# Batch 0 of a fused attention and two-MLP kernel: dividing by the softmax sums before or behind the value products

## The chip, the cores and the metric

The kernel runs on one core of a Trainium2 chip. The metric is the device time in microseconds of one execution. A trace of one profiled execution names the engines PE (TensorE, matrix products; PEld is its weight load), DVE (VectorE), ACT (ScalarE), POOL (GpSimd) and SP (it issues the DMAs here). Each engine works through its own queue strictly in order.

## What is computed

Three stages follow each other, for 2 batches of 768 tokens and a width of 512. The first is an attention over a local window and over block summaries of the keys and values (8 heads of 64). The second is an MLP on shifted tokens with a squared ReLU and a sigmoid gate. The third mixes over tokens and over channels. The change lies in the attention and touches nothing else of this:

```python
scores_all = np.concatenate([scores_l_m, scores_s], axis=-1)   # 768 local (masked) + 24 summaries
scores_all = scores_all - np.max(scores_all, axis=-1, keepdims=True)
a = np.exp(scores_all)
a = a / (np.sum(a, axis=-1, keepdims=True) + 1e-09)
v_all = np.concatenate([v, v_sum], axis=2)
return np.matmul(a, v_all).astype(np.float32)
```

The division may be made on `a`, or on the product with the values: both give the same sum.

## The kernel before

The attention works on tiles of 128 queries, six for each batch, and each tile has two halves `e` of four heads (a head is 64 rows of the 128). In batch 0 a unit of work is one half of one tile, so there are 12 units; in batch 1 a unit is a whole tile. A unit goes through four functions:

- `s_stage`: 8 score products on PE into a PSUM bank (`sp`, line 308); on DVE the mask, with the row's extreme as a by-product (line 321, four for a unit); on ACT the exponential, with the row's sum `den` (line 323, four for a unit).
- `n_stage`: on DVE `den + 1e-9` and its reciprocal (lines 331 and 332); on POOL four multiplications `pe * 1/den` (line 334).
- `t_stage`: four transposes on PE into a bank `pt` (line 340; two such banks) and one copy of the bank to `PT` in SBUF, by DVE in batch 0 and by ACT in batch 1 (lines 345 and 343).
- `v_stage`: 8 value products on PE into the one bank `pv` (line 360); behind the second half of a tile ACT copies `pv` to `xT` (line 367), from which the MLP reads.

`LAGS` says how many units later each of the last three functions of a batch 0 unit is written. A scheduler then sets the final order on each engine, so a change of the code moves work on all of them.

Beside batch 0 the first MLP gets ready. Each of its 16 weight tiles is split into a high and a low part: a shift and a combination on DVE (lines 150 and 156), a scaling and a rounding on ACT (lines 146 and 158), a subtraction on POOL (line 159). `mixed` makes the MLP's input for two tiles of 128 tokens: per 128 channels a product on POOL (`tmp`, line 442) and a combination on DVE (`xk`, line 443), then a rounding on ACT and the low part on DVE (`xl`, line 445). With these PE does the MLP's products (`ko` and `acc`, line 453) between the units of the attention; from batch 1 on they fill its queue. Before batch 1 can score, DVE takes maxima over its keys (`ks`, line 230) and sums over its values (`vrs`, line 252). PE also runs 16 products without use (`spin`, line 532) early on.

Of the kernel before, what the change touches and what calls it, by code (L numbers as in the profile page):

```python
# [9 lines left out]
F32 = mybir.dt.float32  # L10
# [4 lines left out]
ALU = mybir.AluOpType  # L15
# [5 lines left out]
EDGE = WINDOW - 1  # L21
BIG = 1.0e9
KB = 7
LAGS = 1, 2, 3
PEB, PTB, VB = 16, 3, 5
MW = 256
RATIO, NR, RATIO2 = 1.2, 25, 1.8
# [3 lines left out]
SPIN, SPIN_UNITS = 1, 8  # L31
WFIRST = 2
S2COST, S3COST, S4COST = 4, 5, 4
PT_ACT = (1,)
GB = 4
PIN3, PIN4 = 3, 3
PINL = True
# [15 lines left out]
def fused_kernel(ctx, tc, q, k, v, vt, mu, w_k, w_v, w_r, w_t1, w_t2, w_c1, w_c2, out):  # L53
    nc = tc.nc
    B, NT = q.shape[:2]
    S, DM = v.shape[1] - WINDOW * 2, v.shape[2]
    H, D = 8, 64
# [3 lines left out]
    NP = H // 2  # L61
# [14 lines left out]
    def bank(tag, bufs, shape, name):  # L76
        return ps.tile(shape, F32, tag=tag, bufs=bufs, name=name)

    const = pool("const", "left")
    ident = const.tile([128, 128], F32, name="ident")  # L80
# [85 lines left out]
    def in_line(inst):  # L166

        behind(inst, line[-1:])
        line.append(inst)
# [26 lines left out]
    xT = xp.tile([128, KD, B * XB], F32, name="xT")  # L196
    at = pool("at", "right")

    def ahead(n):

        def wrap(fn):
            def run(*args, **kw):
                with tc.high_priority(n) if n else ExitStack():
                    return fn(*args, **kw)
            return run
        return wrap

    state = {}

    def st_of(b):  # L210
        if b not in state:
            state[b] = {"kw": {}, "qT": {}, "vw": {}, "pv": {}}
            state[b]["ks"] = at.tile([128, NP, NB], F32, tag="ks", bufs=2, name="ks")
        return state[b]

# [16 lines left out]
    @ahead(HK)  # L232
    def kw_sums(b, t):
        st = state[b]
        for o in (0, WC - NB):
            nc.gpsimd.tensor_scalar(st["kw"][t][:, :, o:o + NB], st["ks"], 1.0, 1.0, ALU.mult, ALU.mult)
# [17 lines left out]
    @ahead(HR)  # L254
    def v_gather(b):
        st = state[b]
        vp = bank("pt", 2, [128, NP, 128], "vp")
        for p in range(NP):
            nc.tensor.transpose(vp[:NB, p], st["vr"][:, p], ident)
        st["vs"] = at.tile([NB, DM], F32, tag="vs", bufs=1, name="vs")  # L260
        nc.scalar.activation(st["vs"], vp[:NB].rearrange("p g e -> p (g e)"), AF.Copy, scale=1.0 / BLOCK)

    @ahead(HL)
    def vw_load(b, t):
        ws = []
        for half in range(2):
            w = ybuf[:NC, 2 * t + half] if b == 0 else at.tile([NC, DM], F32, tag="vw", bufs=VB, name="vw")
            row, srow = (NB, 0) if half == 0 else (0, NK)
            key = 128 * t + 64 * half
            after(nc.sync.dma_start(w[row:row + NK], v[b, key:key + NK]))  # L270
            ws.append((w, srow))
        st_of(b)["vw"][t] = ws

    def vw_sums(b, t):
        ahead(HV if b or t == 0 else 0)(copy_sums)(b, t)
# [20 lines left out]
    @ahead(HS)  # L296
    def s_stage(b, t, es):
        st = state[b]
        mask = masks[1 if t == 0 else 2 if t == NT - 1 else 0]
        kw, qT = st["kw"][t], st["qT"][t]  # L300
        sps = [bank("s", 2, [128, NP, NC], "sp") for _ in es]
        line.clear()
        for p in range(NP):
            for half in range(2):
                c0 = half * (WC - NC)
                for sp, e in zip(sps[::-1], es[::-1]):
                    r = slice(64 * e, 64 * e + 64)
                    m = nc.tensor.matmul(sp[64 * half:64 * half + 64, p], qT[r, p, 64 * half:64 * half + 64],  # L308
                                         kw[r, p, c0:c0 + NC], start=True, stop=True)
                    if len(es) > 1:  # L310
                        in_line(m)
        if PINL:
            mark.append(m)
        zs = []
        for sp, e in zip(sps, es):
            mn = at.tile([128, NP], F32, tag="mn", bufs=4, name="mn")
            den = at.tile([128, NP], F32, tag="den", bufs=4, name="den")
            P = []
            for p in range(NP):
                pe = at.tile([128, NC], F32, tag="pe", bufs=PEB, name="pe")  # L320
                nc.vector.tensor_tensor_reduce(out=pe, in0=sp[:, p], in1=mask, op0=ALU.add, op1=ALU.min,  # L321
                                               scale=-1.0 / math.sqrt(D), scalar=3.0e38, accum_out=mn[:, p:p + 1])
                nc.scalar.activation(pe, pe, AF.Exp, bias=mn[:, p:p + 1], scale=-1.0, accum_out=den[:, p:p + 1])  # L323
                P.append(pe)
            zs.append({"u": (b, t, e), "P": P, "den": den})
        return zs
# [9 lines left out]
    @ahead(HT)  # L336
    def t_stage(z):
        pt = bank("pt", 2, [128, NP, 128], "pt")
        for p in range(NP):
            nc.tensor.transpose(pt[:NC, p], z["P"][p], ident)  # L340
        z["PT"] = at.tile([NC, NP, 128], F32, tag="PT", bufs=PTB, name="PT")
        if z["u"][0] in PT_ACT:
            nc.scalar.copy(z["PT"], pt[:NC])
        else:
            nc.vector.tensor_copy(z["PT"], pt[:NC])

    @ahead(HV)
    def v_stage(zs):
        b, t, _ = zs[0]["u"]
        st = state[b]  # L350
        if t not in st["pv"]:
            st["pv"][t] = bank("pv", 1, [128, NP, 128], "pv")
        pv = st["pv"][t]
        line.clear()
        for p in range(NP):
            for half in range(2):
                for z in zs[::-1]:
                    e = z["u"][2]
                    h = 2 * p + e
                    m = nc.tensor.matmul(pv[64 * e:64 * e + 64, p, 64 * half:64 * half + 64],  # L360
                                         st["vw"][t][half][0][:, h * D:(h + 1) * D],
                                         z["PT"][:, p, 64 * half:64 * half + 64], start=True, stop=True)
                    if len(zs) > 1:
                        in_line(m)
        if zs[-1]["u"][2] == 1:
            c0 = b * XB + 1 + 128 * t
            nc.scalar.copy(xT[:, :, c0:c0 + 128], pv)

    done_tiles = [0]

    def attention():
        slots = {}
        n0 = 2 * NT
        steps = [(0, t, (e,)) for t in range(NT) for e in range(2)] + [(b, t, (0, 1)) for b in range(1, B) for t in range(NT)]
        for i in range(len(steps) + 1):
            if i < len(steps):
                b, t, es = steps[i]
                zs = s_stage(b, t, es)
                if len(es) == 1:
                    for what, z, lag in zip((n_stage, t_stage, v_stage), (zs[0], zs[0], zs), LAGS):  # L380
                        slots.setdefault(min(i + lag, n0), []).append(((i + lag, lag), what, z))
                else:
                    slots[i + 1] = [((i, 1), n_stage, z) for z in zs] + [((i, 2), t_stage, z) for z in zs] + [((i, 3), v_stage, zs)]
                if i < SPIN_UNITS:
                    spin(SPIN)
                yield 0.95 * len(es)
                if es[-1] == 1 and t + 1 < NT:
                    kw_sums(b, t + 1)
                if t == 0 and es[-1] == 1 - b * (len(es) == 1):
                    if b == 0:  # L390
                        v_gather(b)
                    vw_sums(b, 0)
            for _, what, z in sorted(slots.get(i, ()), key=lambda s: s[0]):
                what(z)
                if what is t_stage:
                    yield 0.43
                elif what is v_stage:
                    yield 0.7 * len(z)
                    done_tiles[0] += len(z) / 2
            if i < len(steps):  # L400
                if 0 in es:
                    if t + 1 < NT and t + 1 not in state[b]["vw"]:
                        vw_load(b, t + 1)
                    if b and t + 2 < NT:
                        q_load(b, t + 2)
                if 1 in es and t + 1 < NT:
                    vw_sums(b, t + 1)
                if b + 1 < B:
                    for e in es:
                        prep_next(b + 1, 2 * t + e)  # L410
# [117 lines left out]
    def spin(n):  # L528

        o = bank("ko", 1, [128, 4, 128], "spin")  # L530
        for _ in range(n):
            after(nc.tensor.matmul(o, ident, ident.unsqueeze(1).to_broadcast([128, 4, 128]), start=True, stop=True))
# [309 lines left out]
```

## Time and profile before

| what | value |
|---|---|
| device time, median of 3 runs | 519.04 us (518.58 to 519.21) |
| the profiled execution, own time | 519.46 us |
| its span in the trace | 517.4 us |
| granted TensorE clock, mean | 0.987 |
| PE busy | 491.9 us (95%) |
| DVE, ACT, POOL busy | 254.8, 203.7, 198.3 us |

The page's second part shows the span in 40 slices of 12.9 us. PE is full from the eighth slice on; before that it has gaps, while DVE and POOL are at 7 to 9 tenths. So the stretch up to about 90 us is one kind of work (batch 0's attention with the weights' splits) and the rest another (PE bound). The trace says at which instruction the one goes over into the other: DVE's first mask of batch 1 at 89.1 us.

### The profile page before, as it was taken

What the parts mean: (1) busy time and instruction counts of PE and PEld (TensorE: products, weight loads), DVE (VectorE), ACT (ScalarE), POOL (GpSimd) and SP (SyncE); (2) the same over time, 40 slices, a digit from 0 to 9 for tenths busy, and PEclk for the clock granted to TensorE, in tenths of its full rate; (3) what the DMA queues carried; (4) which work ended last, traced back from release to release, by engine and by line L of the source; (5) the groups of instructions that cost most, each with busy time, mean ns of one, the idle gap of its engine ahead of it and who ended that gap; (6) DMA issues with size and microseconds to landing.
All of it is one profiled execution on the core that took longest, in us unless ns stands there. A gap on an engine that the chain in (4) does not pass through costs nothing.

```text
span 517.4 us, 7849 instructions
## 1 busy us (share of the span) xinstructions
PE 491.9 (95%) x2968; PEld 398.9 (77%) x2968; DVE 254.8 (49%) x556; ACT 203.7 (39%) x471; POOL 198.3 (38%) x298
## 2 busy tenths in 40 slices
PE   7899687999999999999999999999999999999995
PEld 3457565888888988888867888888888888888884
DVE  3878998733335477587657766343231211311112
ACT  0668445764545645436345344344211110101100
POOL 5587887862655465378423323423100000000000
PEclk9999889899999999999999999999999999999998
DMA  8999941112005700000166351000020000200002
GB/s 269 285 286 353 326 111 33 46 53 84 7 15 209 280 1 1 1 0 2 46 239 236 133 200 42 0 2 0 1 81 1 0 0 1 81 1 0 1 0 81
DMA packets 24196, 45.39 MB, mean 88 GB/s; under 512 B 2112, under 2 KB 11328, under 8 KB 24160
## 3 DMA queue, kind: packets, MB, share of 16 engines
q1 hardware_dynamic: 24160, 44.90, 27.4%
q8 instruction: 23, 0.38, 0.3%
q14 instruction: 13, 0.11, 0.1%
HBM read 41.16 MB, written 3.15 MB: 86 GB/s over the span
## 4 chain that ended last, share of the span: by engine, by line
PE 72%; DVE 10%; DMA 5%; POOL 4%; issue 4%; SPq 2%; ACT 2%; DVEq 0%; POOLq 0%; ACTq 0%
PE o L767 19%; PE go L453 19%; PE ko L453 10%; PE acc L453 9%; PE ro L453 4%; DMA ybuf<-in_v_dram 3%; PE ho L453 3%; PE h L453 2%; PE sp L308 2%; DVE xk L443 2%; DMA wst<-in_moe_w_k_dram 2%; DVE wf L150 2%; PE pv L360 2%; PE pt L340 1%; POOL kl L468 1%
## 5 line engine op out<-in xcount | busy, mean ns | idle before, releaser
L453 PE MATMUL go<-u,w 128*128 128x512 f32 x432 | 106.7, 393 | 0.0
L159 POOL TENSOR_TENSOR w<-wf,w 128x512 fp32r<-128x512 f32 x50 | 66.7, 1337 | 82.4 <-ACT w L158 80.9
L453 PEld LDWEIGHTS go<-u,w 128*128 128x128 f32 x432 | 80.7, 188 | 17.5
L767 PE MATMUL o<-w,gh 128*128 128x512 f32 x288 | 89.0, 395 | 0.0
L682 DVE SCALAR_TENSOR_TENSOR gl<-go,gh 128x512 fp32r<-128x512 f32 x36 | 24.9, 691 | 121.1 <-ACT gh L681 121.0
L453 PE MATMUL ko<-xh,w 128*128 128x256 f32 x384 | 80.5, 295 | 0.0
L681 ACT ACTIVATE gh<-go 128x512 fp32r<-128x512 f32 x36 | 21.6, 599 | 128.7 <-PE go L453 128.7
L453 PEld LDWEIGHTS ko<-xh,w 128*128 128x128 f32 x384 | 64.4, 196 | 2.8 <-issue 0.8
L767 PEld LDWEIGHTS o<-w,gh 128*128 128x128 f32 x288 | 53.9, 188 | 12.1
L453 PE MATMUL acc<-w,kh 128*128 128x512 f32 x192 | 60.1, 400 | 0.6 <-ACT kh L467 0.6
L453 PE MATMUL ko<-xl,w 128*128 128x256 f32 x192 | 56.1, 292 | 2.2 <-DVE xl L445 2.2
L767 PE MATMUL o<-w,gl 128*128 128x512 f32 x144 | 55.4, 394 | 0.0
L158 ACT CAST w<-wf 128x512 fp32r<-128x512 f32 x50 | 31.0, 619 | 54.5 <-DVE wf L156 52.4
L156 DVE SCALAR_TENSOR_TENSOR wf<-wst,wf 128x512 int32<-128x512 int32 x50 | 43.0, 865 | 8.8 <-ACT wst L146 7.0
L323 ACT ACTIVATE pe<-pe,mn 128x120 f32<-128x120 f32 x96 | 36.7, 384 | 25.4 <-DVE mn L321 24.4
L468 POOL TENSOR_TENSOR kl<-rl,kh 128x512 fp32r<-128x512 f32 x24 | 33.1, 1381 | 32.6 <-ACT kh L467 30.9
L442 POOL TENSOR_SCALAR tmp<-xT,oms 128x256 f32<-128x256 f32 x52 | 33.9, 660 | 27.8 <-DVE xk L443 24.6
L334 POOL TENSOR_SCALAR pe<-pe,den 128x120 f32<-128x120 f32 x96 | 39.6, 432 | 12.3 <-DVE den L332 7.1
L443 DVE SCALAR_TENSOR_TENSOR xk<-xT,mus,tmp 128x256 f32<-128x256 f32 x52 | 35.4, 710 | 13.6 <-POOL tmp L442 13.5
L453 PEld LDWEIGHTS acc<-w,kh 128*128 128x128 f32 x192 | 34.4, 188 | 8.0 <-ACT kh L467 1.0
L453 PEld LDWEIGHTS ko<-xl,w 128*128 128x128 f32 x192 | 37.7, 196 | 3.6 <-DVE xl L445 2.4
L453 PE MATMUL acc<-w,kl 128*128 128x512 f32 x96 | 37.3, 404 | 0.5 <-POOL kl L468 0.5
(79 smaller groups left out, 688.6 us busy)
## 6 DMA issues: line engine op xcount, KB each, us to landing
wst<-in_moe_w_ch_dram SPq DMA_DIRECT2D x24, 512.0 KB, 4.8
wst<-in_moe_w_k_dram SPq DMA_DIRECT2D x8, 512.0 KB, 9.6
wst<-in_moe_w_v_dram SPq DMA_DIRECT2D x8, 512.0 KB, 7.1
kw<-in_k_dram SPq DMA_DIRECT2D x12, 320.0 KB, 4.1
wst<-in_moe_w_tok_dram SPq DMA_DIRECT2D x6, 512.0 KB, 7.5
out_dram<-o SPq DMA_DIRECT2D x12, 256.0 KB, 2.1
ybuf<-in_v_dram SPq DMA_DIRECT2D x12, 192.0 KB, 10.9
vw<-in_v_dram SPq DMA_DIRECT2D x12, 192.0 KB, 2.5
```

The source lines that it names most:

```text
L156: nc.vector.scalar_tensor_tensor(wi, top, 3, wi, ALU.logical_shift_left, ALU.bitwise_or)
L158: self.rounded.append(nc.scalar.copy(hi, wf))
L159: nc.gpsimd.tensor_tensor(lo, wf, hi.bitcast(F32), ALU.subtract)
L323: nc.scalar.activation(pe, pe, AF.Exp, bias=mn[:, p:p + 1], scale=-1.0, accum_out=den[:, p:p + 1])
L334: nc.gpsimd.tensor_scalar(z["P"][p], z["P"][p], den[:, p:p + 1], 1.0, ALU.mult, ALU.mult)
L442: nc.gpsimd.tensor_scalar(tmp, xT[:, d, x0 - 1:x0 - 1 + MW], om[:, d:d + 1], 1.0, ALU.mult, ALU.mult)
L443: nc.vector.scalar_tensor_tensor(xk[:, d], xT[:, d, x0:x0 + MW], mu[:, d:d + 1], tmp, ALU.mult, ALU.add)
L453: nc.tensor.matmul(o, l, r, start=(first and i == 0), stop=(last and i == 3 * n - 1))
L468: nc.gpsimd.tensor_tensor(lo, rl, hi.bitcast(F32), ALU.subtract)
L681: nc.scalar.activation(hi, o, AF.Relu)
L682: nc.vector.scalar_tensor_tensor(lo, o, 0.0, hi.bitcast(F32), ALU.max, ALU.subtract)
L767: nc.tensor.matmul(acc[t], l, r, start=(f == 0 and i == 0), stop=(f == nf - 1 and i == 2))
```

## The change

For batch 0 (`LATE`) `n_stage` is no longer called. The exponentials go to the transposes undivided. The two halves of a tile share one tile `dens` of 2 x 4 sums. Behind the value products of a tile DVE adds 1e-9 and takes the reciprocals of all 8 columns at once. PE spreads them: 8 products of a column, repeated 64 times, with the identity give a bank `rb` that holds `1/den` on each head's 64 rows, for each query. `rb` takes one of the two `pt` banks. ACT copies `pv` to `xT` as before, and DVE multiplies `xT` by `rb` in place. The copies `PT` of batch 0's first halves (`e = 0`) go to ACT, those of the second halves stay with DVE; batch 1 keeps all its copies on ACT and its `n_stage`. `LAGS` is one entry shorter.

```diff
-LAGS = 1, 2, 3
+LAGS = 1, 2
+LATE = (0,)
...
-PT_ACT = (1,)
+PT_ACT = ((0, 0), (1, 0), (1, 1))
...
             mn = at.tile([128, NP], F32, tag="mn", bufs=4, name="mn")
-            den = at.tile([128, NP], F32, tag="den", bufs=4, name="den")
+            if b not in LATE:
+                den = at.tile([128, NP], F32, tag="den", bufs=4, name="den")
+            else:
+                if e == 0:
+                    st["den"][t] = at.tile([128, 2, NP], F32, tag="dens", bufs=3, name="dens")
+                den = st["den"][t][:, e]
...
-        if z["u"][0] in PT_ACT:
+        if z["u"][::2] in PT_ACT:
...
-            nc.scalar.copy(xT[:, :, c0:c0 + 128], pv)
+            if b not in LATE:
+                nc.scalar.copy(xT[:, :, c0:c0 + 128], pv)
+            else:
+                den = st["den"].pop(t)
+                nc.vector.tensor_scalar(den, den, 1e-9, None, ALU.add)
+                nc.vector.reciprocal(den, den)
+                rb = bank("pt", 2, [128, NP, 128], "rb")
+                for p in range(NP):
+                    for e in range(2):
+                        nc.tensor.matmul(rb[64 * e:64 * e + 64, p], den[:, e, p:p + 1].to_broadcast([128, D]), ident,
+                                         start=True, stop=True)
+                x = xT[:, :, c0:c0 + 128]
+                nc.scalar.copy(x, pv)
+                nc.vector.tensor_tensor(x, x, rb, ALU.mult)
...
-                    for what, z, lag in zip((n_stage, t_stage, v_stage), (zs[0], zs[0], zs), LAGS):
+                    for what, z, lag in zip((t_stage, v_stage), (zs[0], zs), LAGS):
```

The order on the engines moves with it. POOL's queue in batch 0, before (line numbers are those of each kernel; `pe<-pe,den` is the multiplication of `n_stage`, `w` a weight's low part, `tmp` a part of `mixed`):

```order
L580 TENSOR_SCALAR oms<-mus 128x8
L334 TENSOR_SCALAR pe<-pe,den 128x120 x8
L286 COPY ybuf<-vs 24x512 x5
L334 TENSOR_SCALAR pe<-pe,den 128x120 x4
L159 TENSOR_TENSOR w<-wf,w 128x512
L334 TENSOR_SCALAR pe<-pe,den 128x120 x12
L159 TENSOR_TENSOR w<-wf,w 128x512
```

And the same place of POOL's queue in the changed kernel:

```order
L599 TENSOR_SCALAR oms<-mus 128x8
L287 COPY ybuf<-vs 24x512 x5
L160 TENSOR_TENSOR w<-wf,w 128x512 x3
L461 TENSOR_SCALAR tmp<-xT,oms 128x256 x2
L160 TENSOR_TENSOR w<-wf,w 128x512
L461 TENSOR_SCALAR tmp<-xT,oms 128x256 x2
```

All 48 multiplications of batch 0 are gone from it. On DVE the first multiplication by `rb` stands here, in the changed kernel (tile 0's sums, the copy of its second half's transposes before that):

```order
L151 TENSOR_SCALAR wf<-wst 128x512
L377 TENSOR_SCALAR dens<-dens 128x8
L351 COPY PT<-pt 120x512
L378 RECIPROCAL dens<-dens 128x8
L386 TENSOR_TENSOR xT<-xT,rb 128x4x128
L157 SCALAR_TENSOR_TENSOR wf<-wst,wf 128x512
L327 ISA pe,mn<-sp,mask_163 128x120
```

Behind it in DVE's queue stand a weight and the next unit's masks. On PE, tile 0 of the changed kernel ends so (`pv` are the value products of its two halves, `pt` the transposes of a later unit):

```order
L366 MATMUL pv<-PT,ybuf 64x64 x8
L309 MATMUL sp<-kw,xT 64x120
L366 MATMUL pv<-PT,ybuf 64x64 x8
L382 MATMUL rb<-ident,dens 64x128 x8
L346 MATMUL pt<-ident,pe 120x128 x4
L551 MATMUL spin<-ident 128x512
L309 MATMUL sp<-kw,xT 64x120 x12
```

In the changed kernel 8 units' value products, 4 tiles' `rb` and 9 units' transposes stand in PE's queue ahead of the first `ko` product; before, 10 units' value products and 10 units' transposes did. Of `spin` 15 stand ahead of it, where all 16 did.

## Rows read from the trace of the kernel before

**Rows 1.** The page's head and PE's line of its first part.

```profile
span 517.4 us, 7849 instructions
PE 491.9 (95%) x2968; PEld 398.9 (77%) x2968; DVE 254.8 (49%) x556; ACT 203.7 (39%) x471; POOL 198.3 (38%) x298
```

**Rows 2.** By stretch: length, busy PE, PEld, DVE, ACT, POOL (instructions), PE clock, DMA, GB/s.

```profile
25.00:60.80 35.80, 29.32 (x316) 21.28 (x315) 30.04 (x114) 25.42 (x85) 30.47 (x56) 0.99 1.06 327
60.80:89.10 28.30, 23.71 (x171) 20.03 (x171) 26.58 (x33) 13.61 (x23) 21.56 (x28) 0.89 0.38 96
89.10:517.40 428.30, 418.82 (x2368) 347.87 (x2368) 184.44 (x362) 156.04 (x328) 132.97 (x155) 0.99 0.17 56
```

**Rows 3.** Waits, 36 to 92 us on DVE, 20 to 92 on PE: total, times, longest.

```profile
DVE pe L321 <- PE pt L340: 4.6, 3, 3.4
...
PE pv L360 <- DVE PT L345: 4.2, 4, 1.4
...
PE ko L453 <- DVE xl L445: 2.2, 1, 2.2
```

**Rows 4.** Timelines of POOL, PE and DVE: start, length, instruction, idle time before it.

```profile
30.94 4.82 POOL L334 TENSOR_SCALAR pe<-pe,den 128x120 f32<-128x120 f32 x12
...
35.90 0.60 PE L340 MATMUL pt<-ident,pe 128*120 128x128 f32 x4
...
36.21 0.28 DVE L321 CUSTOM_DVE_ANT_0 pe<-sp,mask 128x120 f32<-128x120 f32 x1 [3.43 <-PE pt L340]
```

**Rows 5.** The chain of waits, 36 to 92 us: start, share of the chain, what.

```profile
36.90 0.61 DVE PT L345
...
46.48 0.08 DVE den L331
...
47.15 0.09 DVE den L332
...
50.88 0.44 DVE xk L443
```

**Rows 6.** Groups by shape: count, busy us, mean ns, idle before; DVE and ACT.

```profile
L626 DVE TENSOR_TENSOR ybuf<-ybuf,ro 128x512 f32<-128x512 f32 x9 | 6.1, 677 | 1.8 <-ACT ro L624 1.8
...
L466 DVE TENSOR_TENSOR rl<-rl 128x512 f32<-128x512 f32 x3 | 3.2, 1065 | 0.0
...
L367 ACT COPY xT<-pv 128x512 f32<-128x512 f32 x6 | 3.5, 579 | 0.9 <-PE pv L360 0.9
```

**Rows 7.** POOL's multiplications of line 334 alone, first stretch: length, busy (count).

```profile
25.00:60.80 35.80, 16.47 (x40) 0.99 1.06 327
```

**Rows 8.** DVE's timeline, then its lines 150 and 443 alone in the first stretch.

```profile
29.29 1.80 DVE L331 TENSOR_SCALAR den<-den 128x4 f32<-128x4 f32 x1
...
37.62 0.42 DVE L150 TENSOR_SCALAR wf<-wst 128x512 int32<-128x512 int32 x1
...
25.00:60.80 35.80, 5.51 (x7) 0.99 1.06 327
...
25.00:60.80 35.80, 2.92 (x4) 0.99 1.06 327
```

**Rows 9.** A weight's two steps on DVE, groups by shape, 0 to 100 us.

```profile
L150 DVE TENSOR_SCALAR wf<-wst 128x512 int32<-128x512 int32 x16 | 12.7, 792 | 1.5 <-POOL w L159 1.5
L156 DVE SCALAR_TENSOR_TENSOR wf<-wst,wf 128x512 int32<-128x512 int32 x16 | 11.8, 743 | 0.2
```

**Rows 10.** PE's timeline: 8 score products, 8 value products, one `spin` (two passes each).

```profile
22.01 1.04 PE L308 MATMUL sp<-kw,xT 64*64 64x120 f32 x16
...
31.69 1.15 PE L360 MATMUL pv<-PT,ybuf 120*64 120x64 f32 x16
...
33.32 1.13 PE L532 MATMUL spin<-ident 128*128 128x512 f32 x2
```

**Rows 11.** The last large load of batch 1: issue on SP, then us from issue to landing.

```profile
59.54 0.48 SPq L244 DMA_DIRECT2D ybuf<-in_vt_dram  x1
...
ybuf<-in_vt_dram SPq DMA_DIRECT2D x2, 768.0 KB, 7.8
```

More of the change, by code (lines that the diff above doesn't have):

```diff
@@ L211, in st_of @@
         if b not in state:
-            state[b] = {"kw": {}, "qT": {}, "vw": {}, "pv": {}}
+            state[b] = {"kw": {}, "qT": {}, "vw": {}, "pv": {}, "den": {}}
             state[b]["ks"] = at.tile([128, NP, NB], F32, tag="ks", bufs=2, name="ks")
```

## The prediction, made before the changed kernel ran

> **What bounds the kernel now.** I read the page first: PE is busy for 95% of the span [rows 1]. The stretches [rows 2] show where its gaps lie; I cut the span at two instructions that both kernels have: the end of DVE's low part `xl` of the first MLP input (60.8 us), without which the MLP's products can't start, and DVE's first mask of batch 1 (89.1 us), which I call T. From T on PE is busy 418.8 of 428.3 us; this is the PE-bound part, and nothing in the change touches its products. From 25.0 us to T DVE is busy 56.6 of 64.1 us. PE counts as busy for 53.0 of them, in the second stretch at a granted clock of 0.89 in the mean, between its two levels of 1.2 and 2.4 GHz. So the time is T plus a PE-bound remainder, and the question is how far T moves, and what is still owed behind it.
>
> Within the first stretch POOL is as full as DVE (30.5 of 35.8 us), and more than half of that, 16.5 us, is the division [rows 7]. It is on the path at least once: twelve multiplications run from 30.94 to 35.76, PE's next transposes start at 35.90 and DVE, which stood for 3.43 us, goes on at 36.21 [rows 4]. In all DVE waits 4.6 us behind such transposes, and PE 4.2 us for DVE's copies `PT` [rows 3]. The chain of waits from 36 us on is mostly DVE work, piece by piece [rows 5].
>
> **DVE's list up to T.** I counted both queues from 25.0 us to the first mask of batch 1; masks, maxima and sums for batch 1, `xl` and the MLP's squares are the same in number.
> - Six of the twelve copies `PT` leave, at 0.61 [rows 5]: -3.7 us.
> - Small steps on `den`: 9 additions and 10 reciprocals before, 5 and 5 (of twice the width) after. At 0.08 and 0.09 [rows 5], with the one addition of 1.80 [rows 8], that was 3.3 us and becomes 0.9: -2.4.
> - Six multiplications by `rb` come. The trace has no such instruction; its bounds are a copy at 0.61 [rows 5] and, above, a product of two tiles in SBUF at 1.07. I take 0.68, the mean of a 128x512 step that also reads one operand from SBUF and one from PSUM [rows 6]: +4.1 (3.7 to 6.4).
> - One weight (0.79 + 0.74 [rows 9]) and two `xk` (0.73 each, 2.92 for four [rows 8]) now stand behind T: -3.0, owed later.
>
> Sum -5.0 us; -1.9 with multiplications at 1.07 and the additions' 1.80 left in (half of that). I keep -5.0.
>
> The addition of 1.80 us was queued while POOL multiplied and split a weight; an uncrowded one takes 0.08 [rows 5, 8]. The Trainium skill ("SBUF — State Buffer", "Who interferes with whom") has a rule for this: VectorE's two-port steps and GpSimd shut each other out for a whole instruction, while a VectorE step with at most one SBUF input stays clear of it. By that rule the multiplication by `rb` runs at the 0.68 end, and the sum is the one taken; by the dearer row it would be 2.3 us more.
>
> **Waits and collisions on DVE.** Of the 4.6 us behind transposes, the 3.43 has POOL's division as its direct cause, and that is gone; the rest I leave: -3.4 (0 to -4.6). Line 150 took 5.51 us for seven, against 0.42 uncrowded: 2.6 too much. `xk` took 2.92 for four, against 0.44: 1.2 too much [rows 5, 8]. Division is 54% of POOL's time there, so I take back 54% of 3.8: -2.0 (0 to -3.8). By DVE alone T moves by -5.0 - 3.4 - 2.0 = -10.4 us.
>
> **PE's list up to the first MLP product.** This caps it. PE was busy 29.3 us from 25.0 to 60.8 [rows 2]. Ahead of the first `ko` the change adds four `rb` of 8 products each, and leaves out two units' value products (1.15 each [rows 10]), one unit's transposes (0.60 [rows 4]) and one `spin` (1.13 [rows 10]). For `rb` the bounds are these. Score products alternate between the two column halves of the array, as `rb` does, and 8 of 120 columns take 1.04. Value products of a unit all use one half, and 8 of 64 columns take 1.15, so 8 of 128 would take 2.30 [rows 10]. I take 1.04, since the alternation is the same: +4.2 - 2.3 - 0.6 - 1.1 = +0.2, and PE, without any gap, gets there at 25.0 + 29.5 = 54.5 us. That is 6.3 us ahead of the 60.8 at which `xl` ended; PE had stood 2.2 us for it [rows 3]. In the second stretch DVE's own list changes by under 0.5 us (three multiplications and two maxima come; weights and `xk` go), so a PE-capped T moves by about -6.5.
>
> The Trainium skill ("TensorEngine Tiling (Array Packing)", "Key Properties") says that tiles of the array work independently, and also that a change of the tiling mode drains the engine. By the first, `rb` costs 1.04 a tile; by the second alone, with its halves in series, 2.30, and the cap would be 59.5. No row shows `rb`.
>
> Between -6.5 and -10.4 I take -8.4. PE's busy time contains modelled ends of matmuls, so 54.5 is on the late side; DVE's sum assumes that nothing new makes it wait, so it is on the early side.
>
> **ACT and the loads.** ACT gets six copies at 0.58 [rows 6], 3.5 us, four of them in a stretch where it is busy 25.4 of 35.8 [rows 2]: covered by its idle time. If that cover fails, each delays a value product, and DVE's multiplication behind it (first rival). In SP's queue one values load of batch 1 moves ahead of three key loads, with the same bytes in all; the last large one is issued at 59.5 and lands 7.8 later, at 67.3 [rows 11], and DVE has some 3 us behind it before T. So no load holds T above 71.
>
> **Behind T.** The 3.0 us owed stand beside batch 1's first units. PE holds products to do meanwhile; the MLP's last block waits for the fifteenth weight. I charge half, +1.5 (0 to 3.0). Two `rb` of 1.04 that follow the first `ko` lie in PE's gaps of the second stretch (4.6 us and the low clock [rows 2]).
>
> **Sum.** -8.4 + 1.5 = -6.9, from the profiled execution's own 519.46: **512.5 us**. The median of the runs is 0.4 lower, so a median of 512.1 would be as much in line. Best ends: -5.0 - 4.6 - 3.8 = -13.4 with nothing owed, 506.1. Worst: only DVE's list, -5.0, with all 3.0 paid back, 517.5.
>
> **Rivals.**
> - *DVE stands at each multiplication by `rb`* (slower). It needs ACT's copy of `pv`, which waits for the value products, which wait for a `PT`. DVE's queue is strict, so a weight and the next masks wait behind it, and with these the next exponentials. If DVE stands for a lap of value products and copy, 1.15 + 0.58, six times, that is 10.4 us: -6.9 + 10.4 = +3.5, 523.0. It decides from 1.15 us a tile. For it: PE already waits 4.2 us for `PT`. Against it: some 4 us of other DVE work stand between a tile's last `PT` and its multiplication.
> - *`rb` runs in series on PE*: 1.26 more for each of six tiles, 7.6 us in a PE queue that caps the first stretch: +0.7, 520.2. The score products speak against it.
> - *The change frees POOL, but POOL was not the path* (it doesn't do what it says): waits and collisions come back under other names, and only the list counts: 517.5. For it: in the second stretch, with no division in it, DVE was just as full.
> - *DVE sets the pace and nothing is owed*: 506.1.
>
> **Chances.** Forecast (508 to 516.5) 0.62; DVE stands 0.11; `rb` in series 0.06; only the list 0.14; the best ends 0.07. From these: faster 0.77 (the forecast less 0.03, nearly all of "only the list", the best ends), within 0.2% 0.09 (half of "in series" among it), slower 0.14; 0.2%, or 1.0 us, is about what a measurement of this kernel can tell from no change. The range for 8 in 10 goes from 506.0 to 517.8.
>
> **What would show it.** Right: POOL's busy time down by some 16 us before T; no wait of DVE for transposes as long as 3.4; `xl` done by 52 to 56 us; T at 79 to 83; `rb` about 1.0 us for 8 products; PE full behind T. Wrong: DVE idle ahead of the multiplications for over 1.2 us a tile; PE's stretch to the first `ko` longer than 35 us; a hole in PE behind T for a weight.

## The result, and the profile after

| what | before | after |
|---|---|---|
| device time, median of 4 runs each | 519.01 us (518.58 to 519.21) | 512.75 us (511.77 to 513.22) |
| span of the profiled execution | 517.4 us | 510.9 us |
| mean granted clock | 0.987 | 0.995 |

The ratio is 0.9878, with a 95% interval from 0.9861 to 0.9895: 6.3 us faster. The prediction said 512.5.

The page's head and the engines' line, as [rows 1]; POOL has lost 16.7 us, PE has gained 96 records, which are the `rb` products in two passes each:

```profile
span 510.9 us, 7961 instructions
PE 494.3 (97%) x3064; PEld 400.1 (78%) x3064; DVE 255.1 (50%) x544; ACT 205.4 (40%) x477; POOL 181.6 (36%) x250
```

The same three stretches as [rows 2], with the same columns. In the changed kernel `xl` (now line 464) ends at 54.2 and the first mask of batch 1 (T) begins at 81.0:

```profile
25.00:54.20 29.20, 27.92 (x345) 21.32 (x341) 26.49 (x102) 26.53 (x87) 13.84 (x15) 1.00 1.06 321
54.20:81.00 26.80, 25.49 (x236) 20.99 (x237) 25.51 (x36) 13.10 (x28) 17.59 (x24) 1.00 0.66 185
81.00:510.90 429.90, 419.68 (x2371) 347.40 (x2369) 191.04 (x366) 157.90 (x333) 139.96 (x158) 0.99 0.17 57
```

So T came 8.1 us earlier, and the part behind it became 1.6 us longer. Up to T, DVE is busy 52.0 us instead of 56.6, and idle 4.0 instead of 7.5. The waits of DVE and PE from 25 us to T (the waiting line, whom it waits for: total, times, longest) show what is left of the idle time. No wait for transposes stands among them ([rows 3] had 4.6 us, with 3.4 at once):

```profile
DVE wf L151 <- POOL w L160: 1.2, 1, 1.2
DVE dens L377 <- ACT pe L329: 1.1, 1, 1.1
DVE wf L157 <- ACT wst L147: 0.8, 1, 0.8
DVE pe L327 <- PE sp L309: 0.7, 1, 0.7
...
PE ko L472 <- DVE xl L464: 1.0, 1, 1.0
PE acc L472 <- ACT kh L486: 0.9, 1, 0.9
```

The new instructions: first PE's timeline of one tile (start, length, instruction), whose 16 records run from 37.42 to 38.68, some beside value products; then all of them as two groups of equal ones (shortest, median and longest in ns, first and last start), where the multiplication takes 0.63 to 0.68 us:

```profile
37.42 0.32 PE L382 MATMUL rb<-ident,dens 128*64 128x128 f32 x1
...
37.64 1.04 PE L382 MATMUL rb<-ident,dens 128*64 128x128 f32 x14
```

```profile
L382 PE MATMUL rb<-ident,dens x96: 271/272/323, 30.3 to 75.7; 128*64 128x128 f32 x96
L386 DVE TENSOR_TENSOR xT<-xT,rb x6: 632/674/679, 33.1 to 80.4; 128x512 f32<-128x512 f32 x6
```

A rule of the Trainium skill ("SBUF — State Buffer", "Who interferes with whom"), by which a DVE step with at most one SBUF input keeps clear of POOL, agrees, though the changed kernel tests it little: none of the six was stretched, but POOL worked beside only one of them. The run below with POOL's load behind the transposes tests it better: POOL worked beside five of the six, and they took 674 to 689 ns.

One difference was not looked for. Stretches of 10 us, from 60 to 70 and from 90 to 100, before (first two rows) and after (columns as above; the eighth number of a row, ahead of the DMA share, is the granted clock):

```profile
60.00:70.00 10.00, 6.67 (x35) 6.40 (x36) 10.00 (x15) 3.23 (x6) 6.86 (x9) 0.69 1.02 267
90.00:100.00 10.00, 9.53 (x83) 7.77 (x84) 8.40 (x39) 7.99 (x34) 7.77 (x11) 0.83 0.26 70
```

```profile
60.00:70.00 10.00, 8.72 (x74) 6.98 (x71) 10.00 (x15) 5.55 (x9) 5.60 (x5) 1.00 1.06 265
90.00:100.00 10.00, 10.00 (x82) 8.05 (x82) 6.72 (x41) 7.34 (x28) 8.60 (x18) 0.85 0.02 9
```

Before, PE stood still between 52 and 61 us three times (1.41 and 1.11 us for `PT`, 2.19 for `xl`) and then ran part of the next stretch at its lower level of 1.2 GHz; after, PE was busy 8.96 us of the ten from 50 to 60, and the clock stayed at 1.00. Ten times one minus the clock, added up over the eight stretches from 20 to 100 us, is 5.1 us before and 1.7 after. That is the most that PE can have lost to the lower level in this window, and I call it the clock loss below.

### The profile page after: what moved, and what is told of

It reads as the page before. It is cut to its first block, busy times and chain, and to the rows that moved or that the text cites. A ratio compares the mean times of both kernels' runs of the same rounds, so it can differ in the third digit from the quotient of the medians.

```text
span 510.9 us, 7961 instructions
## 1 busy us (share of the span) xinstructions
PE 494.3 (97%) x3064; PEld 400.1 (78%) x3064; DVE 255.1 (50%) x544; ACT 205.4 (40%) x477; POOL 181.6 (36%) x250
## 4 chain that ended last, share of the span: by engine, by line
PE 77%; DVE 11%; POOL 3%; issue 3%; ACT 2%; DMA 2%; SPq 1%; DVEq 0%; POOLq 0%; ACTq 0%
PE o L786 19%; PE go L472 19%; PE acc L472 11%; PE ko L472 11%; PE ro L472 5%; PE ho L472 3%; PE h L472 3%; PE pv L366 2%; DMA xT<-in_vt_dram 2%; DVE xk L462 2%; DVE wf L151 2%; DVE wf L157 2%; PE sp L309 2%; PE pt L346 2%; DVE pe L327 1%
## 5 line engine op out<-in xcount | busy, mean ns | idle before, releaser
L472 PE MATMUL ko<-xh,w 128*128 128x256 f32 x384 | 77.2, 287 | 0.7 <-ACT w L159 0.6
L472 PEld LDWEIGHTS ko<-xh,w 128*128 128x128 f32 x384 | 61.8, 188 | 4.6 <-issue 1.3
L472 PE MATMUL ko<-xl,w 128*128 128x256 f32 x192 | 54.9, 286 | 1.0 <-DVE xl L464 1.0
L462 DVE SCALAR_TENSOR_TENSOR xk<-xT,mus,tmp 128x256 f32<-128x256 f32 x52 | 37.1, 739 | 7.1 <-POOL tmp L461 7.0
L472 PEld LDWEIGHTS ko<-xl,w 128*128 128x128 f32 x192 | 36.2, 188 | 2.5 <-DVE xl L464 1.3
L485 DVE TENSOR_TENSOR rl<-rl 128x512 f32<-128x512 f32 x24 | 19.2, 799 | 31.8 <-ACT rl L484 31.5
```

Source lines behind the costliest of these rows:

```text
L462: nc.vector.scalar_tensor_tensor(xk[:, d], xT[:, d, x0:x0 + MW], mu[:, d:d + 1], tmp, ALU.mult, ALU.add)
L472: nc.tensor.matmul(o, l, r, start=(first and i == 0), stop=(last and i == 3 * n - 1))
L485: nc.vector.tensor_tensor(rl, rl, rl, ALU.mult)
```

## Experiments

Two theories. **The loop**, the prediction's: the division lay in a loop from DVE over POOL and PE back to DVE; without it DVE and PE come to the first MLP product sooner, and PE's own queue then caps the gain. **The list**: POOL's path was not what mattered; the gain is that DVE has less to do, or that the code's new order (the shorter lags) suits the scheduler better. The expectations of the next two runs have letters of their own: A is DVE's list and PE's queue together, B that POOL's division was the cost and the copies are by the way, C that the copies are what gained.

Every edit below also makes the scheduler put other work in another order, so each difference holds the edit and a new order together.

Each run is compared by its ratio to runs of the kernel before on the same chip; "as time" below is that ratio times 519.0, with its interval, and the changed kernel is then 512.7 (511.8 to 513.6).

**One part of the change at a time.** The division moved, with all twelve copies left on DVE:

```diff
-PT_ACT = ((0, 0), (1, 0), (1, 1))
+PT_ACT = ((1, 0), (1, 1))
```

> The changed kernel with all of batch 0's copies PT back on DVE: only the division is moved. Theory A (DVE's list and PE's queue share the first stretch): DVE gets back six copies at 0.61 us, 3.7 us, of which PE's queue, which ends the stretch at 54 us in the changed kernel, hides a part: 514 to 516.5 us. Theory B (POOL's division was the cost, the copies are by the way): within 1 us of the changed kernel's 512.75, so 512 to 513.7. Theory C (the copies on ACT are what gained): 518 or more.

Measured: 0.9998 (0.9959 to 1.0037), as time 518.9 (516.9 to 520.9). No gain at all: by itself that is C's range, 518 or more, and not A's or B's. The other half, the kernel before with six copies on ACT:

```diff
-PT_ACT = (1,)
+PT_ACT = ((0, 0), (1, 0), (1, 1))
...
-        if z["u"][0] in PT_ACT:
+        if z["u"][::2] in PT_ACT:
```

> The kernel before with batch 0's first copies PT on ACT and nothing else. Theory A: DVE's list is 3.7 us shorter, but its transposes still stand behind POOL's multiplications, so a part of it comes through: 516 to 518.5 us. Theory B: no gain, 518.5 to 519.5. Theory C: 512.5 to 514.5.

Measured: 0.9933 (0.9905 to 0.9960), as time 515.5 (514.1 to 516.9), between C's range (512.5 to 514.5) and A's (516 to 518.5). None of the three gives both runs. The kernel before with the short lags alone:

```diff
-LAGS = 1, 2, 3
+LAGS = 1, 1, 2
```

> The kernel before with one edit: the transposes follow their unit by one step and the value products by two (before, two and three), as in the changed kernel; POOL still divides and the copies stay where they were. If the shorter lag is what shifts the work, a good part of the gain comes with it: 514 to 517. If the division has to be away for a short lag to pay, DVE and PE now stand behind POOL's twelve multiplications of each unit, one unit earlier than before: no gain or a loss, 519 to 523.

Measured: 1.0020 (0.9987 to 1.0054), as time 520.0 (518.3 to 521.8). The lags alone give nothing. Lags and copies together, that is, the whole change but the division:

> The kernel before with the shorter lags and with six of the twelve PT copies on ACT: all of the change but the division, which stays on POOL ahead of the transposes. The difference to the changed kernel is the division alone. By the prediction the division gives the 3.4 us wait and 2.0 us of collisions less 0.7 of DVE steps, some 4 to 6 us: this kernel at 516 to 519. If POOL's load and its delay cost nothing, as the run with dummy multiplications ahead of the transposes reads, this kernel is within 1.5 us of the changed one, 511 to 514.

Measured: 0.9945 (0.9924 to 0.9966), as time 516.2 (515.1 to 517.2). From here to the changed kernel only the division moves, and that is worth 3.5 us. With the copies still on DVE it was worth 1.1 (520.0 to 518.9), less than the intervals can tell from nothing. The copies gave 3.5 alone and 3.8 on top of the short lags. That the two halves help each other is thus likely, but at the edge of what these intervals show. In this kernel DVE and PE still wait behind POOL's division (of PE's 2.5 us, 1.7 in batch 0); one of DVE's waits, then one of PE's, 20 to 100 us:

```profile
DVE pe L321 <- PE pt L340: 2.6, 2, 1.8
...
PE pt L340 <- POOL pe L334: 2.5, 3, 1.3
```

**POOL's load, and POOL's loop.** First 48 multiplications by 1.0 on POOL, the old number, put where nobody on the path waits for them, behind each unit's transposes:

```diff
+        if z["u"][0] in LATE:
+            for p in range(NP):
+                nc.gpsimd.tensor_scalar(z["P"][p], z["P"][p], 1.0, 1.0, ALU.mult, ALU.mult)
```

> The changed kernel, with 48 POOL multiplications by 1.0 of the same shape as the division's, in batch 0, each behind the transposes that read its tile: nobody waits for them but a later user of the buffer. POOL is as loaded as before, the latency is not there. If POOL's time itself and its collisions with DVE were the gain: 517 to 520 us. If the wait of the transposes was: 512.5 to 514.5. My sum had 2.0 us for the collisions and 3.4 for the wait: 514.0 to 515.5.

Measured: 0.9919 (0.9889 to 0.9948), as time 514.8 (513.2 to 516.3), 2.1 more than the changed kernel. That is what the prediction's 2.0 us of collisions would have given, but not for that reason: from 20 to 100 us the weights' two steps on DVE and `xk` took 29.6 us here (12.2, 9.4 and 8.0), and 33.7 in the changed kernel. The same lines ahead of the transposes, hanging on the exponentials alone:

> The changed kernel, with 48 POOL multiplications by 1.0 in batch 0 between the exponentials and the transposes, so that the transposes wait for them as they did for the division. Against the run with the same multiplications behind the transposes this shows the latency alone. By my sum both terms come back, 2.0 + 3.4 us: 517 to 519 us. If only POOL's load counts: the same as the run behind the transposes, within 1 us. If neither counts: 512.5 to 513.5.

Measured: 0.9859 (0.9787 to 0.9932), as time 511.7 (508.0 to 515.5), from three runs, and without a trace of any of them. The interval excludes that POOL's load and its delay between exponential and transpose by themselves cost the 5.4 us that the prediction gave to waiting and collisions. It doesn't show that they cost nothing: two of the runs took 511.6 at a mean clock of 0.999, the third 515.5 at 0.991, where an execution of the changed kernel at 0.992 took 512.8. What this run lacks of the old path is DVE: before, POOL's factor came out of DVE's queue. So the same again with two DVE steps ahead of POOL:

```diff
+        if z["u"][0] in LATE:
+            one = at.tile([128, NP], F32, tag="one", bufs=4, name="one")
+            nc.vector.tensor_scalar(one, z["den"], 0.0, 1.0, ALU.mult, ALU.add)
+            nc.vector.reciprocal(one, one)
+            for p in range(NP):
+                nc.gpsimd.tensor_scalar(z["P"][p], z["P"][p], one[:, p:p + 1], 1.0, ALU.mult, ALU.mult)
```

> The changed kernel with the old path put back as ballast: for each unit of batch 0 DVE makes a column of ones out of the sums (an addition and a reciprocal, 0.17 us, 2 us in all) and POOL multiplies the exponentials by it ahead of the transposes, 48 multiplications, 16 us. Unlike the earlier run, whose multiplications hung on the exponentials alone, these also wait for DVE's queue. If the way DVE to POOL to PE and back to DVE is what the division cost (the prediction's 3.4 us of waiting and 2.0 of collisions), the time rises by 4 to 7 us, to 517 to 520. If only work on DVE counts, it rises by its 2 us: 513.5 to 515.5.

Measured: 1.0090 (1.0052 to 1.0128), as time 523.7 (521.7 to 525.7): 11 us more. Waits like those that the change had removed are back. DVE's from 20 to 100 us, then POOL's multiplications (line 349) from 15 to 100 us, which stood 7.2 us for DVE's reciprocal:

```profile
DVE pe L327 <- PE pt L352: 4.3, 1, 4.3
DVE pe L327 <- PE sp L309: 3.7, 3, 1.6
```

```profile
L349 POOL TENSOR_SCALAR pe<-pe,one 128x120 f32<-128x120 f32 x48 | 19.4, 422 | 9.9 <-DVE one L347 7.2 <-ACT pe L329 1.3 <-DVE dens L383 0.8
```

The 4.3 us are not POOL's alone: its multiplications ended at 35.4 and the transposes began at 37.4, behind other products in PE's queue.

The added DVE steps in that window (count, busy us, mean ns, idle before), and the stretch from 18 to 28 us:

```profile
L346 DVE TENSOR_SCALAR one<-dens 128x4 f32<-128x4 f32 x11 | 3.9, 352 | 0.4 <-ACT pe L329 0.3
L347 DVE RECIPROCAL one<-one 128x4 f32<-128x4 f32 x11 | 1.9, 171 | 0.1
```

```profile
18.00:28.00 10.00, 10.00 (x48) 5.24 (x47) 8.69 (x51) 8.58 (x35) 7.22 (x15) 0.53 1.08 321
```

The steps were taken at 2 us and took 5.8, the additions 352 ns in the mean beside POOL. The run agrees with the loop theory, but does not isolate the loop. From 18 to 28 us the clock stood at 0.53, where the changed kernel has 1.00 with PE 9.49 us busy; that is up to 4.7 us in this execution, and the run doesn't say why the clock was low there. The eight executions of this kernel show what such a loss goes with: three at a mean clock of 0.991 took 522.2 to 522.7, three at 0.982 (the one with the trace among them) 526.4 to 527.2. At nearly the changed kernel's clock it is thus still some 10 us slower. The order moved as well: one more unit's value products and transposes stand ahead of the first `ko` than in the changed kernel, and the low part `xl` of the first MLP input ends at 65.4 us instead of 54.2. How the 10 us divide between the loop, the DVE steps and the order is not shown.

**What the new division costs.** The changed kernel without additions, reciprocals, `rb` and multiplications in batch 0:

```diff
-                den = st["den"].pop(t)
...
-                nc.vector.tensor_tensor(x, x, rb, ALU.mult)
+                nc.scalar.copy(xT[:, :, c0:c0 + 128], pv)
```

> The changed kernel without its division of batch 0: no addition, no reciprocal, no product rb, no multiplication, so batch 0's x stays undivided. It prices what the new division itself still costs. If, as the prediction has it, DVE's and PE's lists set the start together, six multiplications of 0.65 and the small steps leave DVE (some 5 us) and four rb of 1.04 leave PE ahead of the first MLP product (4.2 us): the time falls by about 4 us below the changed kernel, to 508 to 510. If the start is set by something else (the steps that feed a unit in turn, or the order in which the scheduler puts them), the time stays within 1 us, at 512 to 514.

Measured: 0.9811 (0.9768 to 0.9855), as time 509.2 (507.0 to 511.5): the new division costs some 3.5 us. Against this kernel the one with lags and copies, which has the old division, needs 7.0 us more (516.2): moving it halved its price. Is it DVE's or PE's share? Each multiplication issued twice:

```diff
+                nc.vector.tensor_tensor(x, x, rb, ALU.mult)
```

> The changed kernel with each multiplication by rb issued twice, so batch 0's x is divided twice: six more DVE steps of 0.65 us, 3.9 us in all, with nothing else changed on any engine. If DVE's amount of work is what bounds the start, ahead of T and behind it until about 100 us, the time rises by 3 to 5 us, to 516 to 518. If PE's queue caps the start, as the prediction has it, DVE has room for a part of it and the time rises by 0 to 2 us, 512.5 to 515.

Measured: 0.9847 (0.9806 to 0.9887), as time 511.1 (508.9 to 513.1), so with 4 us more work on DVE no loss can be seen. The second multiplications are there (line 387, six at 0.68):

```profile
L387 DVE TENSOR_TENSOR xT<-xT,rb x6: 673/680/687, 33.0 to 83.4; 128x512 f32<-128x512 f32 x6
```

This speaks against the list theory, by which DVE's amount of work sets the time, but doesn't exclude it. Contrary to the expectation other things did change: the scheduler's order differs from 34 us on, one more unit's value products and transposes stand ahead of the first `ko`, T comes at 76.1 instead of 81.0, and the clock loss is 0.0 instead of 1.7. The 3.5 us of the new division may then be PE's, which has six times 1.04 us of `rb` or more; that is inferred, not measured by itself. Against it: in the kernel without the division PE stands 2.6 us for `xl`, which ends at 51.3, so DVE still ends that stretch. The order of the `rb` products, the four of one column half first, then the four of the other:

```diff
-                for p in range(NP):
-                    for e in range(2):
+                line.clear()
+                for e in range(2):
+                    for p in range(NP):
...
+                        in_line(m)
```

> The changed kernel with the eight products rb of a tile ordered by column half: four of the one half, then four of the other, instead of in turns. If products overlap only when neighbours in PE's queue go to different halves, a tile's eight take about 2.3 us instead of 1.04; 1.26 us on each of the four tiles ahead of the first MLP product is 5 us on PE, and if PE caps that stretch the time rises by 3 to 5 us, to 516 to 518. If the halves overlap in any order, the eight stay at about 1.0 and the time within 1 us of the changed kernel (512 to 514). If rb costs 2.3 and the time still doesn't move, PE is not the cap.

Measured: 0.9969 (0.9941 to 0.9996), as time 517.4 (515.9 to 518.8): 4.7 us more. But a tile's `rb` takes 1.58 us here, against 1.26 in the changed kernel, not 2.3:

```profile
50.43 1.58 PE L383 MATMUL rb<-ident,dens 128*64 128x128 f32 x16
```

Six times 0.32 is 1.9 us. The forecast number came for the wrong reason: PE reached the first MLP product earlier than in the changed kernel (`xl` at 52.5), with one tile's `rb` and one unit's score products fewer ahead of it, T lay at 80.8, and the rest was lost behind T, where PE stood still four times for 0.7 to 1.8 us between 71 and 91 us and the clock was 0.83 from 80 to 100.

**Looking for a faster one.** All twelve copies on ACT:

```diff
-PT_ACT = ((0, 0), (1, 0), (1, 1))
+PT_ACT = ((0, 0), (0, 1), (1, 0), (1, 1))
```

> The changed kernel with all twelve PT copies of batch 0 on ACT: 3.7 us less for DVE (six at 0.61), 3.5 us more for ACT. If DVE's amount of work bounds the start, the time falls by 2 to 4 us, to 509 to 511. If PE's queue caps it, nothing is gained: 512 to 513.5. If ACT, now with all the copies beside the exponentials, becomes the engine that is waited for, the time rises by 1 to 4 us: 514 to 517.

Measured: 0.9937 (0.9908 to 0.9967), as time 515.7 (514.2 to 517.3), 3 us worse. PE's waits from 20 to 100 us, and the stretch from 40 to 50 us, where ACT is now full:

```profile
PE pt L346 <- DVE xT L386: 3.3, 2, 2.3
...
PE pv L366 <- ACT xT L385: 0.9, 1, 0.9
```

```profile
40.00:50.00 10.00, 7.33 (x100) 6.01 (x96) 10.00 (x37) 10.00 (x36) 6.60 (x8) 1.00 1.03 356
```

`rb` holds one of the two `pt` banks until DVE has multiplied; when that comes late, PE's next transposes wait for the bank. It is a near relative of the prediction's first rival, with PE as the engine that stands instead of DVE. And the changed kernel without the eight spins between the first units:

```diff
-SPIN, SPIN_UNITS = 1, 8
+SPIN, SPIN_UNITS = 1, 0
```

> The changed kernel without the eight spin products that PE does for nothing between the first units, 1.13 us each. If PE's queue caps the stretch to the first MLP product, up to 8 us come free on it and the time falls by 2 to 5 us, to 508 to 511, as long as the granted clock stays at 1.00 there. If PE is not the cap, the time stays at 512 to 514. If the idle time that the spins filled lets the granted clock fall ahead of 50 us, the time rises by 2 to 6 us: 515 to 519.

Measured: 0.9966 (0.9941 to 0.9990), as time 517.2 (515.9 to 518.5), 4.5 us worse for 9 us less of PE work. From 12 to 16 and from 16 to 36 us, without (first) and with the spins:

```profile
12.00:16.00 4.00, 1.91 (x34) 1.57 (x34) 1.99 (x4) 0.00 (x0) 2.85 (x12) 0.99 1.05 366
...
16.00:36.00 20.00, 19.29 (x156) 15.33 (x156) 12.27 (x60) 14.84 (x58) 5.32 (x7) 0.50 1.08 304
```

```profile
12.00:16.00 4.00, 2.93 (x34) 1.75 (x34) 1.86 (x3) 0.00 (x0) 2.85 (x12) 1.00 1.04 336
...
16.00:36.00 20.00, 19.00 (x189) 12.43 (x189) 16.07 (x78) 16.50 (x65) 6.49 (x8) 1.00 1.08 281
```

PE is busy in both, but at 1.2 GHz without the spins: 156 records instead of 189 in the same 20 us. Before the fall it had been busy 1.9 of 4 us, with the spins 2.9. So this run can't tell whether PE's queue is the cap.

**The clock over all these kernels.** The clock loss (eight stretches, 20 to 100 us) beside the time, for the kernels that hold the change's division: doubled multiplications 0.0 us and 511.1; the change itself 1.7 and 512.7; all copies on ACT 3.4 and 515.7; halves in turn 3.4 and 517.4; POOL's load behind the transposes 5.1 and 514.8; division without copies 5.1 and 518.9; the loop put back 7.1 and 523.7; no spins 13.4 and 517.2, with 9 us less on PE. Mostly the time goes with the loss, and over a wider span than the loss itself. It is a correlation: gaps on PE cost time, and in most of these runs also come ahead of the lower level. The kernels outside this list break it: the one without any division lost 5.1 and was the fastest (509.2), the one with the copies alone lost 8.5, more than the 5.1 of the kernel before, and gained 3.5. No run here changes the clock alone, but executions of one kernel differ in it. Of the kernel before, the ones with the highest mean clock (0.988) took 518.2 to 519.6; of the changed kernel, the one with the lowest (0.992) took 512.8. Their clocks are some 2 us of loss apart, their times 5.4 to 6.8. So if the lower level costs no more time than its loss, about half of the gain or more is not the clock's.

## Why the prediction was right, and where it wasn't

**The total** came out at 512.75 against 512.5, by the waits and PE's queue as predicted and in part by luck (below), with T at 81.0 (79 to 83 was said), `xl` done at 54.2 (52 to 56) and 1.6 us paid back behind T (1.5). The signs that it named are there: the 3.4 us wait is gone, POOL lost 20.6 us up to T, `rb` costs about what score products do, no DVE idle time stands ahead of any of the six multiplications.

**DVE's list and waits.** Predicted -5.0 for the list and -2.0 for collisions, both busy time, and -3.4 for waits. DVE's busy time up to T fell by 4.6 and its idle time by 3.5. The multiplication was taken at 0.68 and took 0.67 in the median. The prices of 0.08 and 0.09 for the small steps were pieces of the chain of waits [rows 5]; the steps themselves take 0.17 and 0.18 in the median, so their term was nearer -3.1 than -2.4. The list missed one item: the five copies `ybuf` on DVE, done by 25.0 us before (2.2 us), now stand at 24.1 to 27.5, 3.1 us of them behind the point where both lists begin:

```profile
24.11 3.42 DVE L285 COPY ybuf<-vs 24x512 f32<-24x512 f32 x5 [1.26 <-ACT vs L262]
```

That the waits went because the division left the loop is supported twice, not proved: they are still there with copies and lags alone, and waits of the kind come back when the loop does.

**Collisions with POOL: right in its own terms, wrong for DVE as a whole.** The step "I take back 54% of 3.8" named line 150 and `xk` in the first stretch. Their rows of after, to be read beside [rows 8], give -1.8 where -2.0 was said:

```profile
25.00:54.20 29.20, 4.06 (x7) 1.00 1.06 321
25.00:54.20 29.20, 2.54 (x4) 1.00 1.06 321
```

But DVE met POOL in other places instead. From 20 to 100 us line 150 fell from 12.7 to 10.1 us for its 16 ([rows 9]); the weights' other step and `xk`, which had 11.8 and 7.6, now take 14.3 and 9.3, for the same 16 and 12. DVE's groups of after in that window:

```profile
L157 DVE SCALAR_TENSOR_TENSOR wf<-wst,wf 128x512 int32<-128x512 int32 x16 | 14.3, 892 | 1.0 <-ACT wst L147 0.8
L151 DVE TENSOR_SCALAR wf<-wst 128x512 int32<-128x512 int32 x16 | 10.1, 632 | 1.2 <-POOL w L160 1.2
L462 DVE SCALAR_TENSOR_TENSOR xk<-xT,mus,tmp 128x256 f32<-128x256 f32 x12 | 9.3, 772 | 0.0
```

Together that is 1.6 us more. This and the copies `ybuf` are the main reasons why DVE's account came to -4.6 - 3.5 = -8.1, which is T's move, and not to -10.4. It did no harm to the total, because the value taken was -8.4, halfway to PE's cap. No step of the working gives that half, so that it hit -8.1 is in part luck: up to `xl` the gain was 6.6 us, as PE's cap had it (6.3), and the other 1.5 came in the second stretch, where the prediction expected under 0.5 from DVE's list and gave the clock no price.

**PE's cap: near, for a part of the reason.** PE was to be full up to 54.5. It was busy 27.9 us from 25.0 to 54.2, 1.6 less than the 29.5 of the sum, and stood 1.0 us for `xl` at the end. So DVE's `xl` still ended the stretch. The price of `rb`, 1.04, is 1.26 from first to last record, with value products still running beside it; the choice between 1.04 and 2.30 was right. The 2.30 itself was too dear: doubling the 1.15 of the value products doubles the 0.22 of their last pass too, and at the 0.11 us by which the passes of one half follow each other in the run with halves in turn, 16 in series would take some 2.0 (an estimate).

**Behind T** the half that was charged fits, but T itself is a poorer measure than the prediction took it for. The copies alone had T at 73.8, the division alone at 77.0, both earlier than the change's 81.0, and both ended later: behind T they needed 440.5 and 439.7 us, against 428.3 before. The scheduler had only put other work behind the cut. A cut is a fair account between two kernels when the list of what crosses it is made, as it was for T (at 25.0 us it missed the copies `ybuf`); it ranks no variants.

**The lower clock level was left out.** The prediction read 0.89 in the second stretch and gave it no price. Its loss fell by 3.4 us, all of it ahead of T, and that is a part of the 6.3 in another account, not on top of -8.4: a PE without gaps both did more and kept its clock. By the executions compared above about half of the 6.3 or more is not the clock's; the exact division stays open.

**The rivals.** DVE never stood at the multiplications in the changed kernel; in four of the variants with six copies on ACT it did, for 0.8 to 1.5 us in all. `rb` in series is excluded by its own rows. "Only the list counts" (517.5) doesn't fit the division's 3.5 us on top of the copies, since by the list alone (-2.4 for small steps, +4.1 for multiplications) it would have cost 1.7; the doubled multiplications speak against it too, as far as another order allows. ACT's cover held for six copies and failed for twelve. That the division without the copies gives nothing fits neither the loop nor the list; the expectation's C gave the number, but not the run with the copies alone. That kernel reaches `xl` at 51.3 us, earlier than the change, and loses it again behind T, with a PE gap of 2.6 us that ends at 93.6 and the clock at 0.83 in three of five stretches from 50 to 100 us. What in the order makes these gaps isn't settled.

## What to carry to other kernels

Look for work that sits in a loop across several strict queues, and not only for the engine that is full: here 16 us of POOL work that didn't hang on DVE cost 2.1 us in one place and nothing measurable in another, while the division whose factor came through DVE's queue cost 7.0 against none at all, and 3.5 once it stood behind the products. That the loop makes this difference is likely, but the order moved with every edit. A division by a sum that can be made behind the product leaves such a loop, and here paid only with six of the copies on ACT; with none or all of them there the time was worse. Where a scheduler sets the order, judge a change by the whole time and by PE's gaps and granted clock, since one marked instruction can come earlier while the kernel gets slower.

## What the runs showed of the chip that was not expected

Eight products without use, 9 us of PE time, went with a time 4.5 us shorter: without them PE ran at 0.50 of its clock from 16 to 36 us although it was busy 19.3 of these 20 us. And products that alternate between the two column halves are not the only ones that overlap: four of one half, then four of the other took 1.58 us for 8, where 16 passes in series would take some 2.0; the second half's first pass starts at 50.92, the first half's last at 51.24.

PE also pays when products of different shape take turns. In the changed kernel one transposes' pass on the whole width and two value passes on one half alternate here:

```profile
35.98 0.33 PE L366 MATMUL pv<-PT,ybuf 120*64 120x64 f32 x2
36.24 0.33 PE L346 MATMUL pt<-ident,pe 128*120 128x128 f32 x1
36.50 0.33 PE L366 MATMUL pv<-PT,ybuf 120*64 120x64 f32 x2
```

A transposes' pass and two value passes take 0.52 us so; among their own kind passes start 0.11 and 0.06 us apart, which would make 0.23. The value products and `rb`, both 64 columns wide, mix without such a step (37.42 to 37.64 above). The Trainium skill ("TensorEngine Tiling (Array Packing)", "Key Properties") has tiles work in parallel and a change of mode drain the engine; both orders of `rb` show the first, and these steps agree with the second, though no run here was made to test it. The two halves of `rb` have one shape, so a change of mode gave no reason for the 2.30 in the prediction.
